# One PSUM bank in place of two for the phase sums, half a granule kept in the other, and a reordered first step and tail

## The chip, the core and the metric

The kernel runs on one core of a Trainium2 chip. The metric is the time of one execution in microseconds, as the device measures it. The engines are named as in the profile: PE (TensorE matmuls, PEld its weight loads), DVE (VectorE), ACT (ScalarE), POOL (GpSimd) and SP (SyncE, which here only issues transfers). Each engine works through its own instructions in the order in which the program puts them, and waits on semaphores for the others.

## The reference

Two branches are added to the input. A is an attention layer with a recurrent memory: 64 segments of 32 rows go through it one after the other, each behind 8 memory rows, which are the first 8 output rows of the segment before. B sends the two rows with the largest router score through a gated MLP.

```python
def _A_ref(x, mem0, Wq, Wk, Wv, Wo, seg_len):
    ...
    for s in range(n_seg):
        xs = x[:, s * seg_len:(s + 1) * seg_len, :].copy()
        h = jnp.concatenate([mem, xs], axis=1)
        q = jnp.einsum('btd,dhe->bhte', h, Wq)
        k = jnp.einsum('btd,dhe->bhte', h, Wk)
        v = jnp.einsum('btd,dhe->bhte', h, Wv)
        scores = jnp.einsum('bhqe,bhke->bhqk', q, k) * scale
        scores = jnp.where(mask[None, None], scores, -1000000000.0)
        p = _softmax(scores, axis=-1)
        o = jnp.einsum('bhqk,bhke->bhqe', p, v)
        o = jnp.einsum('bhte,hed->btd', o, Wo)
        mem = o[:, :M, :].copy()
        outs.append(o[:, M:, :])
...
xn = _layernorm(x, axis=-1)
return x + _A_ref(xn, A_mem0, A_Wq, A_Wk, A_Wv, A_Wo, A_seg_len) + _B_ref(xn, B_w_r, B_w_gate, B_w_up, B_w_down)
```

x is 1 x 2048 x 1024 in bf16, with 32 heads of 128; the MLP has 3584 hidden columns. The last 8 rows of a segment (called left rows here) and the first 24 are handled apart, since the left rows' queries, keys and values don't depend on the memory and can be computed for all segments at once, in the first step.

## The kernel before

The weights Wq, Wk, Wv and Wo are cut into 64 granules of 128 partitions by 2048 columns (512 KB). 44 of them stay in SBUF (`wres`, `W8A`, `W8B`, `XLT`); two and a half lie in PSUM, in the four tiles KEPT (granules 0, 7 and part of 27), and are copied into SBUF buffers BK just before they are read (`bring_back`, L404). The other 17 (`streamed`) are fetched again in every segment through five slots: `fetch` (L375) issues the transfer of the granule five places ahead when a granule has been read.

A segment's step runs six phases (L742): Q, K of the first 16 heads, Q, K of the second 16, V of the first, V of the second. A phase sums eight granules into a PSUM tile PSm (L745), four matmuls at a time on four column groups of PE; a group of four is the unit of pace in what follows. ACT copies PSm into XB (L754) or VM (L770), and the pool psA has two banks, so that the next phase begins in the other one at once. Three groups into the next phase PE turns XB (L632) into the buffer BT, from where ACT and DVE copy it to QT or KT (L637, L642).

The scores of a half (L650, L652) go to the bank BS after group 6 of phases 2 and 4. DVE adds the mask and subtracts the maximum (L659 to L665), ACT takes the exponential (L669), DVE divides by the sum and transposes (L674 to L685): `exponent` and `soften`. `attend` (L703, L706) multiplies by V, twice for each half; its sums lie in BT and, for the first half, in the second half of the bank that will hold WO. ACT copies them to OT and OTL (L712, L714). Then L350 puts the residual into WO, and 16 pairs of heads are projected into it (L789), with the attends of the second half ahead of pairs 5 and 8. L819 copies WO to XN, PE turns it into the memory columns of the next segment's ST (L340, L364), and the next step begins.

The places where such pieces of work go are written by hand: `hook(p, kc, fn)` runs fn after group kc of phase p. Within an engine the program keeps that order.

In the first step PE also computes the left rows' Q, K and V (`left_qk` L495, `left_v` L522), from PSUM tiles of the same two banks; the router's scores are 16 tiles of work on DVE (`router_tile`, L263 and L265), started after phase 0; the two rows with the largest scores are then picked and loaded (`router_top`, `route`) after phase 2. In the tail the left rows' attention is projected in two blocks (`left_rows_out`, L865), and the MLP's weights come in 46 pieces: 32 of gate and up, read by `gate_up` (L894), and 14 of down (L921). Each piece read frees the room for another.

Of the kernel before, what the change touches and what calls it, by code (L numbers as in the profile page):

```python
# [22 lines left out]
KEPT_HERE = (FIRST_KEPT, NEXT_KEPT, HALF_KEPT)  # L23
NEG = -30000.0
# [5 lines left out]
def kernel(  # L30
# [68 lines left out]

    def granule_out(t, g):  # L100
        return t[:, :] if g < 48 else t.rearrange("p (hh d) -> p hh d", hh=2)
# [7 lines left out]
    psA = ctx.enter_context(tc.tile_pool(name="psA", bufs=2, space=PSUM))  # L109
# [10 lines left out]
    wsc = {g: dram.tile([P, 2048], BF16, name=f"wsc{g}") for g in streamed}  # L120
# [106 lines left out]
    def left_turns():  # L227
        for t in range(4):
            PX = psA.tile([P, 1024], BF16, tag="acc", name="PX").rearrange("p (k t) -> p k t", k=KC)
# [56 lines left out]
    def route():  # L286
        T = home(hx, [P, 2048], BF16, "RT2")
        xs, T = T[0:2, 0:1024], T[:, 1024:2048]
        for c in range(2):
            v = nc.gpsimd.value_load(I8[0:1, c:c + 1], min_val=0, max_val=S - 1)  # L290
            routed_rows.append(v)
            nc.gpsimd.dma_start(out=xs[c:c + 1, :], in_=x2[bass.ds(v, 1), :])
        mv = T[0:2, 24:26].rearrange("p (t c) -> p t c", t=1)
# [81 lines left out]
    def fetch():  # L375
# [6 lines left out]
        else:  # L382
            nc.sync.dma_start(out=t[:, :], in_=wsc[g][:, :])
# [6 lines left out]
    def keep(g, t):  # L390
        for c, K in KEPT_COLS[g].items():
# [3 lines left out]
            XK = one.tile([P, 512], BF16, tag="bx", name="XK")  # L395
# [17 lines left out]
    def copy_block(g):  # L413
        nc.gpsimd.dma_start(out=granule_out(wsc[g], g), in_=granule_dram(g))
# [73 lines left out]
    def left_qk(mat, half, Gs, between, h0=0, h1=16):  # L488
# [3 lines left out]
        for h in range(h0, h1):  # L492
            PSG = psA.tile([P, 512], F32, tag="acc", name="PSG")
# [22 lines left out]
    def left_v(half, Gs):  # L516
        VG = home(hm, [P, 2048], BF16, "VG")
        for b in range(4):
            for jq in range(4):
                PSV = psA.tile([P, 512], F32, tag="acc", name="PSV")  # L520
# [22 lines left out]
    def left_done(p):  # L543
# [3 lines left out]
        if p == 0:  # L547
            spread(1, NT)
            for t in range(NT):
                router_tile(t)  # L550
        elif p == 1:
            router_out()
# [3 lines left out]
        elif p == 2:  # L556
            router_top()
            routed.append(route())
# [62 lines left out]
    for s in range(NSEG):  # L621
# [115 lines left out]

        for p, (mat, half) in enumerate(PHASES):
            PSm = psA.tile([P, 512], F32, tag="acc", name="PSm")
# [12 lines left out]
            if mat < 2:  # L752
                XB = one.tile([P, 512], BF16, tag=("bE", "kt")[mat], name="XB")
                nc.scalar.copy(out=XB[:, :], in_=PSm[:, :])  # L754
                hooks.setdefault((p + 1, 3), []).insert(0, lambda m=mat, h=half, b=XB: transposes(m, h, b))

                if s == 0:
                    Gs = [Gv_ for _, Gv_ in behind]
                    kept = (x for g_, Gv_ in behind if g_ in KEPT_COLS for x in keep(g_, Gv_))
                    if p == 0:  # L760
                        left_qk(mat, half, Gs, kept, 8, 13)
                        sd_rows(MV[:, 1:NT, :], VE[:, 1:NT])
                    elif p == 1:
                        left_qk(mat, half, Gs, kept, 0, 1)
                        nc.gpsimd.tensor_copy(out=GATE, in_=gathered[0][:, 0, 128:132])
                        copy_blocks(6)
                    left_qk(mat, half, Gs, kept, (13, 1)[p] if p < 2 else 0)
            else:
                VM[half] = one.tile([P, 512], BF16, tag="bA", name="VM")
                nc.scalar.copy(out=VM[half][:, :], in_=PSm[:, :])  # L770
# [6 lines left out]
        if s == 0:  # L777
            nxt["wo"] = psA.tile([P, 512], F32, tag="acc", name="WO")

        WO = nxt["wo"]  # L780
# [104 lines left out]
    GU = psA.tile([P, 512], F32, tag="acc", name="GU")  # L885
# [16 lines left out]
    early = len(pieces) + FC // 2 - len(moe)  # L902
# [60 lines left out]
```

## Time and profile before

| | |
|---|---|
| median of 3 runs | 1857.16 us (1852.51 to 1863.57) |
| profiled execution | 1853.95 us |
| its span, first to last instruction | 1852.3 us |
| PE busy | 1554.8 us, 84% |
| DVE busy | 880.0 us, 48% |
| ACT busy | 772.9 us, 42% |
| POOL busy | 320.9 us, 17% |
| moved by DMA | 678.50 MB, mean 366 GB/s |
| mean granted TensorE clock | 0.98 |

Busy shares are means over a first step of some 245 us, 63 like steps, and a tail of some 90 us. Rows of a timeline give the start in us, the duration, the engine, the line of the kernel, the operation with its output and inputs, their shapes, and in brackets how long the engine stood idle before it and who released it. A matmul's row lasts longer than its place in the pipeline: the next one starts before it ends.

### The profile page before, as it was taken

The page shows a single profiled execution, that of the slowest core. Times are in us where ns is not written, and L with a number is a line of the kernel's source. Part 1 is how long each engine was busy: PE and PEld are TensorE (multiplying, and loading weights), DVE is VectorE, ACT ScalarE, POOL GpSimd, SP SyncE. Part 2 cuts the span into 40 slices and gives each one's busy share as a digit, 9 for nine tenths or more (in the row PEclk, how much of TensorE's full clock was granted, in tenths as well). Part 3 has the DMA queues.
Part 4 walks back from the last instruction along what each step waited for, and adds up shares of the span by engine and source line. Part 5 has one row for each costly group of instructions (what it writes and reads, how often), then busy time and mean ns, then how long its engine had stood idle before and what let it go on. Part 6 is the DMA issues. An engine that isn't in the chain of part 4 may idle for free. (4 is left out here: it accounts for less than half of the span.)

```text
span 1852.3 us, 70387 instructions
## 1 busy us (share of the span) xinstructions
PE 1554.8 (84%) x30370; PEld 828.2 (45%) x30370; DVE 880.0 (48%) x2711; ACT 772.9 (42%) x2017; POOL 320.9 (17%) x592
## 2 busy tenths in 40 slices
PE   6879978888888888888888888888888888888888
PEld 3334434444444444444444444444444444444465
DVE  6721135555554444555555555545555455555420
ACT  3232134444444444444444444444444444444400
POOL 1120211111111111111111111111111111111200
PEclk9989989999999999999999999999999999999988
DMA  9692899999999999999999999999999999999996
GB/s 357 236 332 81 263 334 393 397 392 393 380 395 382 382 365 393 390 386 381 388 397 394 380 392 394 393 361 394 395 396 396 391 394 394 398 395 392 390 365 224
DMA packets 223288, 678.50 MB, mean 366 GB/s; under 512 B 46848, under 2 KB 54320, under 8 KB 222976
## 3 DMA queue, kind: packets, MB, share of 16 engines
q1 hardware_dynamic: 196768, 623.79, 87.8%
q0 software_dynamic: 24192, 46.54, 7.5%
q8 instruction: 237, 3.88, 0.8%
q10 hardware_dynamic: 2016, 3.67, 0.6%
q14 instruction: 75, 0.61, 0.1%
HBM read 652.90 MB, written 29.89 MB: 369 GB/s over the span
## 5 line engine op out<-in xcount | busy, mean ns | idle before, releaser
L745 PE MATMUL PSm<-wres,ST 128*32 128x512 bf16 x6400 | 500.8, 383 | 0.0
L745 PEld LDWEIGHTS <-ST 128*32 128x32 bf16 x12288 | 313.6, 96 | 333.1 <-issue 90.8
L745 PE MATMUL PSm<-g,ST 128*32 128x512 bf16 x3084 | 307.2, 384 | 32.9 <-DMA g<-wsc 27.2
L406 ACT COPY BK<-KEPT 128x512 bf16<-128x512 bf16 x315 | 189.3, 601 | 180.4 <-PE WO L789 70.4
L789 PEld LDWEIGHTS <-OT 128*32 128x32 bf16 x8192 | 209.0, 97 | 93.1 <-issue 77.4
L754 ACT CAST XB<-PSm 128x512 bf16<-128x512 f32 x256 | 150.3, 587 | 119.9 <-PE PSm L745 118.2
L642 DVE COPY KT<-BT 128x512 bf16<-128x512 bf16 x128 | 51.8, 405 | 287.4 <-PE BT L632 287.4
L789 PE MATMUL WO<-W8B,OT 128*32 128x256 bf16 x4096 | 185.7, 276 | 0.0
L745 PE MATMUL PSm<-W8A,ST 128*32 128x512 bf16 x2048 | 182.9, 380 | 0.0
L789 PE MATMUL WO<-g,OT 128*32 128x256 bf16 x2560 | 131.0, 278 | 58.9 <-DMA g<-wsc 52.3
L587 POOL DMA_DIRECT2D QKL<-ql_d x63 | 46.5, 739 | 750.3 <-ACT OTL L714 735.7
L823 POOL DMA_DIRECT2D out_dram<-XN x256 | 130.4, 525 | 183.3 <-DVE XN L819 183.0
L770 ACT CAST VM<-PSm 128x512 bf16<-128x512 f32 x128 | 80.2, 626 | 113.2 <-PE PSm L745 113.1
L406 DVE COPY BK<-KEPT 128x512 bf16<-128x512 bf16 x189 | 80.2, 424 | 72.5 <-ACT BK L406 36.9
L495 PE MATMUL PSG<-XLT,wres 128*128 128x512 bf16 x352 | 99.6, 385 | 12.1 <-ACT XB L754 12.1
L632 PEld LDWEIGHTS <-XB 128*128 128x128 bf16 x1024 | 58.0, 98 | 108.5 <-ACT XB L754 101.4
L632 PE MATMUL BT<-IDENT,XB 128*128 128x128 bf16 x1024 | 101.9, 222 | 3.6
L674 DVE TENSOR_REDUCE DN<-BS 128x8 f32<-128x320 f32 x128 | 62.9, 492 | 84.1 <-ACT BS L669 84.1
L637 ACT COPY QT<-BT 128x512 bf16<-128x512 bf16 x128 | 75.0, 586 | 54.8 <-PE BT L632 52.6
L659 DVE TENSOR_TENSOR BS<-BS,CT 128x96 f32<-128x96 f32 (+1 forms) x256 | 59.6, 233 | 76.5 <-PE BS L652 72.0
L745 PE MATMUL PSm<-BK,ST 128*32 128x512 bf16 x567 | 76.5, 389 | 22.2 <-DVE ST L364 22.2
L819 DVE CAST XN<-WO 128x256 bf16<-128x256 f32 x64 | 27.2, 425 | 137.3 <-PE WO L789 137.3
(171 smaller groups left out, 2278.2 us busy)
## 6 DMA issues: line engine op xcount, KB each, us to landing
g<-wsc SPq DMA_DIRECT2D x1071, 512.0 KB, 6.3
ql_d<-GA POOLq DMA_DIRECT2D x16, 512.0 KB, 5.7
QKL<-ql_d POOLq DMA_DIRECT2D x63, 128.0 KB, 6.3
MW<-in_B_w_gate_dram SPq DMA_DIRECT2D x16, 448.0 KB, 7.9
MW<-in_B_w_down_dram SPq DMA_DIRECT2D x14, 512.0 KB, 9.8
wres<-in_A_Wk_dram SPq DMA_DIRECT2D x12, 512.0 KB, 10.3
MW<-in_B_w_up_dram SPq DMA_DIRECT2D x12, 448.0 KB, 8.5
XP<-in_A_x_dram SPq DMA_DIRECT2D x8, 512.0 KB, 10.2
```

The costliest lines, as they stand in the source:

```text
L406: copy(out=back[g][c], in_=KEPT_COLS[g][c])
L495: nc.tensor.matmul(PSG[:, :], lhsT=part(Gs[kc], h // 4)[:, P * (h % 4):P * (h % 4 + 1)], rhs=XLT[:, :, kc, :], start=(kc == 0), stop=(kc = ...
L632: nc.tensor.transpose(out=PTq[:, il, :, :].rearrange("p j r -> p (j r)"), in_=XB[:, il * P:(il + 1) * P], identity=IDENT[:, :])
L637: nc.scalar.copy(out=QT[half][:, :, :], in_=pv)
L642: nc.vector.tensor_copy(out=KT[half][:, :, 0:32], in_=pv)
L659: nc.vector.tensor_tensor(out=S4, in0=S4, in1=m, op=ALU.add)
L674: nc.vector.tensor_reduce(out=DN[:, :], in_=S8, axis=AX.X, op=ALU.add)
L745: nc.tensor.matmul(PSm[32 * jq:32 * jq + 32, :], lhsT=ST[:, kc, :], rhs=part(Gv, jq), start=(kc == 0), stop=(kc == KC - 1), tile_position= ...
L754: nc.scalar.copy(out=XB[:, :], in_=PSm[:, :])
L770: nc.scalar.copy(out=VM[half][:, :], in_=PSm[:, :])
L789: nc.tensor.matmul(PS[32 * g:32 * g + 32, 0:256], lhsT=lhs(h), rhs=Gv[:, D * hs + 256 * g:D * hs + 256 * (g + 1)], start=False, stop=(last ...
L823: nc.gpsimd.dma_start(out=out2[s * SEG:s * SEG + XM, 256 * g:256 * (g + 1)], in_=OB[32 * g:32 * g + XM, :])
```

## The change

Five things change.

1. The banks of psA become two named tiles, a0 and a1. In the first step the sums alternate between them as before; from the second step on, all six phases and WO use a0 (`accumulator`).
2. PSm is copied out in two halves of 256 columns, the first by ACT, the second by DVE, for XB as for VM. Some work for PE moves between the phases (`between`): Q's transposes go from the middle of K's phase to its end, the scores of the first half behind phase 2. The attends of the first half move from groups 3 and 6 of phase 5 to groups 5 and 7, and their sums use BS in every step.
3. From the second step on, a1 holds half of granule 45 (KEPT4). Only the other half, 128 x 1024, is copied to scratch and streamed; in each step DVE and ACT copy the kept columns into the same slot (`kept_piece`, in phase 4). In the first step the two kept blocks are turned twice by PE, with ACT between, to get into PSUM (`keep`).
4. In the first step the router's 16 tiles move from behind phase 0 to behind the third head of phase 1; the router's output row, the loading of the two rows and their normalisation move one place later as well, `route` to behind the eighth head of phase 3.
5. In the tail, 20 instead of 26 of the 32 gate and up pieces are read ahead of the second block of left rows.

```diff
+HALF_STREAMED = 45
+    def accumulator(shape, dtype, name, both):
+        sums_of[0] = (sums_of[0] + 1) % 2 if both else 0
+        return psA.tile(shape, dtype, tag=f"a{sums_of[0]}", name=name)
...
-    psA = ctx.enter_context(tc.tile_pool(name="psA", bufs=2, space=PSUM))
+    psA = ctx.enter_context(tc.tile_pool(name="psA", bufs=1, space=PSUM))
...
-            nc.sync.dma_start(out=t[:, :], in_=wsc[g][:, :])
+            nc.sync.dma_start(out=t[:, 0:columns(g)], in_=wsc[g][:, :])
...
+    def kept_piece(c, copy):
+        t = [t for q, t in queued if q == HALF_STREAMED][0]
+        copy(out=t[:, 512 * c:512 * (c + 1)], in_=KEPT_COLS[HALF_STREAMED][c])
...
-                    if s > 0:
-                        nxt["wo"] = psA.tile([P, 512], F32, tag="acc", name="WO")
...
-                sums[half] = [BS[:, 0:4 * NK] if half or s == 0 else nxt["wo"][:, 256:256 + 4 * NK], OPB]
+                sums[half] = [BS[:, 0:4 * NK], OPB]
...
-        hook(2, 6, lambda: scores(0))
         if s > 0:
-            hook(2, 7, lambda: bring_back(HALF_KEPT, 3, "kt", nc.scalar.copy))
+            hook(3, 0, lambda: bring_back(HALF_KEPT, 3, "kt", nc.scalar.copy))
+            hook(4, 1, lambda: kept_piece(2, nc.vector.tensor_copy))
+            hook(4, 2, lambda: kept_piece(3, nc.scalar.copy))
         hook(3, 4, exponent)
         hook(3, 4, lambda: soften(0))
...
-        hook(*((5, 0) if s else (4, 7)), exponent)
-        hook(*((5, 0) if s else (4, 7)), lambda: soften(1))
-        hook(5, 3, lambda: attend(0, 0))
-        hook(5, 6, lambda: attend(0, 1))
+        if s > 0:
+            hook(5, 0, exponent)
+            hook(5, 0, lambda: soften(1))
+        hook(5, 5, lambda: attend(0, 0))
+        hook(5, 7, lambda: attend(0, 1))
+        hook(4, 6, lambda: scores(1))
+
+        def between(p):
+            if p == 2:
+                scores(0)
+            elif p == 4 and s == 0:
+                exponent()
+                soften(1)
+            elif p % 2 == 1:
+                turned_q.pop()()
...
-            PSm = psA.tile([P, 512], F32, tag="acc", name="PSm")
+            PSm = accumulator([P, 512], F32, "PSm", s == 0)
...
-                nc.scalar.copy(out=XB[:, :], in_=PSm[:, :])
-                hooks.setdefault((p + 1, 3), []).insert(0, lambda m=mat, h=half, b=XB: transposes(m, h, b))
+                nc.scalar.copy(out=XB[:, 0:256], in_=PSm[:, 0:256])
+                nc.vector.tensor_copy(out=XB[:, 256:512], in_=PSm[:, 256:512])
+                turn_it = lambda m=mat, h=half, b=XB: transposes(m, h, b)
+                if mat == 0:
+                    turned_q.append(turn_it)
+                else:
+                    hooks.setdefault((p + 1, 3), []).insert(0, turn_it)
+                if p > 0:
+                    between(p)
...
-                nc.scalar.copy(out=VM[half][:, :], in_=PSm[:, :])
+                nc.scalar.copy(out=VM[half][:, 0:256], in_=PSm[:, 0:256])
+                nc.vector.tensor_copy(out=VM[half][:, 256:512], in_=PSm[:, 256:512])
...
+            KEPT.append(psA.tile([P, 1024], BF16, tag="a1", name="KEPT4"))
...
-    early = len(pieces) + FC // 2 - len(moe)
+    early = len(moe)
```

How the instructions stand on the engines is shown at three places; the words in brackets are the semaphores of the engines (or DMA queues) that an instruction waits for, without the value. Line numbers of the changed kernel lie some 15 to 40 above those of before.

PE, from phase 0 to phase 1 of a later step: the last rows of phase 0, which read a granule kept in PSUM (BK), and the first of phase 1 (a resident granule). Before:

```order
L745 MATMUL PSm<-BK,ST 32x512 [waits DVE_49]
L745 LDWEIGHTS ST
L745 MATMUL PSm<-BK,ST 32x512 [waits Activation_49]
L745 LDWEIGHTS ST
L745 MATMUL PSm<-wres_217,ST 32x512 [waits PE_49]
```

and in the change:

```order
L771 MATMUL PSm<-BK,ST 32x512 [waits DVE_49]
L771 LDWEIGHTS ST
L771 MATMUL PSm<-BK,ST 32x512 [waits Activation_49]
L771 LDWEIGHTS ST
L771 MATMUL PSm<-wres_217,ST 32x512 [waits DVE_49]
```

The first matmul of phase 1 waited for PE itself and now waits for DVE; the first matmuls of phases 2 to 5 and of WO do the same.

DVE, from the maximum of the first half's scores (NM, BS) through the softmax (DN, PT, PL) to the K copy of the second half (KT). Before:

```order
L665 TENSOR_TENSOR BS<-BS,NM 128x320 [waits DVE_49]
L674 TENSOR_REDUCE DN<-BS 128x8 [waits Activation_49]
L675 RECIPROCAL DN<-DN 128x8 [waits DVE_49]
L680 TENSOR_TENSOR PT_2469<-BS,DN 128x256 [waits DVE_49,PE_49]
L681 TENSOR_TENSOR PL<-BS,DN 128x4x2x8
L684 STREAM_TRANSPOSE PT_2469<-PT_2469 128x256 [waits DVE_49]
L685 STREAM_TRANSPOSE PT_2469<-PL 128x256 [waits DVE_49]
L642 COPY KT<-BT 128x16x32 [waits PE_49,Activation_49]
```

and in the change:

```order
L680 TENSOR_TENSOR BS<-BS,NM 128x320 [waits DVE_49]
L689 TENSOR_REDUCE DN<-BS 128x8 [waits Activation_49]
L690 RECIPROCAL DN<-DN 128x8 [waits DVE_49]
L695 TENSOR_TENSOR PT_2493<-BS,DN 128x256 [waits DVE_49,PE_49]
L696 TENSOR_TENSOR PL<-BS,DN 128x4x2x8
L699 STREAM_TRANSPOSE PT_2493<-PT_2493 128x256 [waits DVE_49]
L700 STREAM_TRANSPOSE PT_2493<-PL 128x256 [waits DVE_49]
L781 CAST XB<-PSm 128x256 [waits Activation_49]
L434 COPY g<-KEPT_2063 128x512 [waits DMAHW7_49,DMAHW2_49,DMAHW1_49]
L657 COPY KT<-BT 128x16x32 [waits DVE_49,PE_49,Activation_49]
```

Two instructions have come between the softmax and the K copy: DVE's half of phase 3's sums, which waits for ACT, and the copy of a kept piece of granule 45.

DVE, the same place for the second half. Before:

```order
L664 TENSOR_REDUCE NM<-BS 128x8 [waits DVE_49]
L665 TENSOR_TENSOR BS<-BS,NM 128x320 [waits DVE_49]
L674 TENSOR_REDUCE DN<-BS 128x8 [waits Activation_49]
L675 RECIPROCAL DN<-DN 128x8 [waits DVE_49]
L680 TENSOR_TENSOR PT_2583<-BS,DN 128x256 [waits DVE_49]
```

and in the change:

```order
L679 TENSOR_REDUCE NM<-BS 128x8 [waits DVE_49]
L680 TENSOR_TENSOR BS<-BS,NM 128x320 [waits DVE_49]
L813 CAST VM<-PSm 128x256 [waits DMASW3_49,Activation_49]
L689 TENSOR_REDUCE DN<-BS 128x8 [waits Activation_49]
L690 RECIPROCAL DN<-DN 128x8 [waits DVE_49]
L695 TENSOR_TENSOR PT_2617<-BS,DN 128x256 [waits DVE_49]
```

DVE's half of VM[0], the sums of phase 4, now stands between the maximum and the softmax; the other half of VM, of phase 5, stands behind the softmax.

More of the change, by code (lines that the diff above doesn't have):

```diff
@@ L118, with columns @@
     ol_d = [dram.tile([16, P, XL * H], BF16, name=f"ol_d{t}") for t in range(4)]
-    wsc = {g: dram.tile([P, 2048], BF16, name=f"wsc{g}") for g in streamed}
+    def columns(g):
+        return 1024 if g == HALF_STREAMED else 2048
+    wsc = {g: dram.tile([P, columns(g)], BF16, name=f"wsc{g}") for g in streamed}
     r_d = dram.tile([1, S], BF16, name="r_d")
@@ L292, in route @@
             nc.gpsimd.dma_start(out=xs[c:c + 1, :], in_=x2[bass.ds(v, 1), :])
+        routed.append(T)
+    def route():
+        T = routed.pop()
+        xs, T = T[0:2, 0:1024], T[:, 1024:2048]
         mv = T[0:2, 24:26].rearrange("p (t c) -> p t c", t=1)
@@ L413, in copy_block @@
     def copy_block(g):
-        nc.gpsimd.dma_start(out=granule_out(wsc[g], g), in_=granule_dram(g))
+        src = granule_dram(g)
+        nc.gpsimd.dma_start(out=granule_out(wsc[g], g), in_=src if g >= 48 else src[:, 0:columns(g)])
+    def kept_piece(c, copy):
+        t = [t for q, t in queued if q == HALF_STREAMED][0]
+        copy(out=t[:, 512 * c:512 * (c + 1)], in_=KEPT_COLS[HALF_STREAMED][c])
     to_copy = list(streamed)
@@ L492, in left_qk @@
         for h in range(h0, h1):
[L493 removed]
+            PSG = accumulator([P, 512], F32, "PSG", True)
             for kc in range(KC):
@@ L546, in left_done @@
                 fetch()
[L547 to L552, printed above, removed]
+        if p == 1:
             area("big0", [P, 8, 2048], "W8A")
@@ L557, in left_done @@
             router_top()
-            routed.append(route())
+            route_rows()
         elif p == 3:
```

47 lines of the change are left out of this document (31 added, 16 removed).

## The prediction

> **What bounds the kernel now.** I read the page first, then the line L819, which runs once a segment, the waits, and the timelines of PE, ACT and DVE over whole steps.
>
> ```profile
> span 1852.3 us, 70387 instructions
> g<-wsc SPq DMA_DIRECT2D x1071, 512.0 KB, 6.3
> ...
> L819 DVE CAST XN<-WO x64: 423/425/426, 245.1 to 1762.1; 128x256 bf16<-128x256 f32 x64
> ...
> 300.00:1700.00 1400.00, 1182.01 (x26140) 630.09 (x26136) 710.99 (x2274) 652.77 (x1750) 258.45 (x467) 1.00 1.01 389
> ...
> PE WO L789 <- DMA g<-wsc: 52.3, 100, 2.2
> PE PSm L745 <- DMA g<-wsc: 27.2, 69, 1.2
> ```
>
> L819 ends each segment's step, so a step is (1762.1 - 245.1) / 63 = 24.08 us; the first step and its set-up take 245 us, the tail 90. In the third row (busy times of PE, PE loads, DVE, ACT, POOL, then clock, DMA share, GB/s) the DMA engines are never idle and move 389 GB/s, 9.37 MB a step, of which the 17 granules are 8.9. The transfers set the pace, but by little, as one step on PE shows:
>
> ```profile
> 1019.05 0.40 PE L745 MATMUL PSm<-BK,ST 128*32 128x512 bf16 x4 [0.35 <-DVE ST L364]
> 1021.58 0.39 PE L745 MATMUL PSm<-BK,ST 128*32 128x512 bf16 x3
> 1025.33 0.40 PE L632 MATMUL BT<-IDENT,XB 128*128 128x128 bf16 x4
> 1025.66 0.40 PE L745 MATMUL PSm<-wres,ST 128*32 128x512 bf16 x4
> 1026.10 0.39 PE L745 MATMUL PSm<-wres,ST 128*32 128x512 bf16 x4
> 1026.32 0.21 PE L650 MATMUL BS<-KT,QT 128*32 128x40 bf16 x4
> 1032.01 0.21 PE L650 MATMUL BS<-KT,QT 128*32 128x40 bf16 x4 [0.45 <-DVE KT L642]
> 1036.41 0.31 PE L350 MATMUL WO<-XS,IDENT 128*32 128x256 bf16 x4 [0.21 <-ACT OTL L714]
> 1044.20 0.40 PE L745 MATMUL PSm<-BK,ST 128*32 128x512 bf16 x4 [0.35 <-DVE ST L364]
> 1050.68 0.21 PE L650 MATMUL BS<-KT,QT 128*32 128x40 bf16 x4
> 1056.37 0.21 PE L650 MATMUL BS<-KT,QT 128*32 128x40 bf16 x4 [0.69 <-DVE KT L642]
> ```
>
> I cut the step into four: A from phase 0 to the first scores (L650), B to the second scores, C to the residual matmul (L350), D to the next phase 0. B is 5.69 us in both steps here (1026.32 to 1032.01, 1050.68 to 1056.37), and a wait for DVE ends it, not one for a DMA: a chain through ACT and DVE, from the scores over the softmax to the next scores, that no transfer shortens. The two waits for g add up to 79.5 us, 1.3 us a step. So there is at most a few us a step between the transfers' pace and that of the chain PE-ACT-DVE, and what lengthens the chain by more comes out in full.
>
> **The change, part by part.** *The handoff.* From step 1 on all phases and WO share the bank a0. The first matmul of each phase waits for DVE, whose half of the copy waits for ACT alone; since nothing else tells DVE that the matmuls are done, ACT's half is what it waits for. The two halves run one behind the other.
>
> ```profile
> 1022.08 0.59 ACT L754 CAST XB<-PSm 128x512 bf16<-128x512 f32 x1 [1.94 <-PE PSm L745]
> 1038.11 0.27 ACT L712 CAST OT<-BS 128x128 bf16<-128x128 f32 x1 [1.02 <-PE BT L706]
> ```
>
> ACT takes 0.59 us for 512 columns and 0.27 for 128; on the line between them, 0.38 for 256. DVE's 256 columns are L819's 0.425. Gaps: matmul end to ACT 0.11 (1021.58 + 0.39 to 1022.08); ACT to DVE 0.04 and DVE to PE 0.06 (rows below: 1028.96 + 0.43 to 1029.43; 1031.57 + 0.38 to 1032.01). From the last group of four matmuls to the next phase: 0.39 + 0.11 + 0.38 + 0.04 + 0.43 + 0.06 = 1.41 us, where the pace was 0.22 (1026.10 to 1026.32). Each free handoff costs PE 1.19 us. Not shown is a bank read by both engines; were the halves side by side, a handoff would take 0.42 less (0.38 + 0.04), and that end is kept as a rival.
>
> [...]
>
> *DVE's queue.* DVE works in order, and its half of phase 3's copy stands behind the whole softmax of the first half, its half of VM[0] behind the mask and maximum of the second. These are the prices:
>
> ```profile
> 1026.82 0.27 DVE L659 TENSOR_TENSOR BS<-BS,CT 128x96 f32<-128x96 f32 x1 [0.56 <-PE BS L652]
> 1028.17 0.50 DVE L665 TENSOR_TENSOR BS<-BS,NM 128x320 f32<-128x320 f32 x1
> 1028.96 0.43 ACT L669 ACTIVATE BS<-BS 128x320 f32<-128x320 f32 x1
> 1029.43 0.49 DVE L674 TENSOR_REDUCE DN<-BS 128x8 f32<-128x320 f32 x1 [0.76 <-ACT BS L669]
> 1031.20 0.45 DVE L685 STREAM_TRANSPOSE PT<-PL 128x256 bf16<-128x256 bf16 x1
> 1031.57 0.38 DVE L642 COPY KT<-BT 128x512 bf16<-128x512 bf16 x1
> 1034.86 0.49 DVE L674 TENSOR_REDUCE DN<-BS 128x8 f32<-128x320 f32 x1 [0.49 <-ACT BS L669]
> 1035.96 0.21 DVE L681 TENSOR_TENSOR PL<-BS,DN 128x64 bf16<-128x64 f32 x1
> ```
>
> Masks begin 0.50 us after the scores and take 1.85 (1026.82 to 1028.67); exponential 0.43 with 0.04 on either side; softmax 2.22 (1029.43 to 1031.65), of which BS is free after 1.31 (1034.86 to 1036.17).
>
> A, new: 24 groups x 0.22 = 5.28, one set of K transposes 0.33 (1025.33 to 1025.66; Q's now lie in the handoff of phase 1), two handoffs 2.38. **A = 8.0** (7.27 here, 6.48 in the next step).
>
> B, new: phase 2's copy into XB takes the buffer that the scores still read as QT, so ACT starts at 0.50 and DVE ends at 1.35; phase 3 starts at 1.41 and would be over near 3.4. Masks 1.35 to 3.20, exponential to 3.67, softmax 3.71 to 5.93, DVE's half of phase 3 to about 6.28 (DVE starts the next independent instruction 0.08 early, 1031.57 against 1031.65), phase 4 at 6.34. PE stands still for almost 3 us. Then seven groups 1.54, transposes 0.33, K copied meanwhile: **B = 8.25**, 2.56 more. The copy of granule 45's kept piece (DVE, a copy of 512 columns, 0.38 by the KT row; ACT 0.6) lies in the first groups of phase 4 where DVE and ACT are free: nothing, or 0.4 a step without that cover.
>
> C, new: masks end at 2.35, DVE's half of VM[0] at 2.78, phase 5 at 2.84 (it followed at once before). Six groups to 4.16; BS, which now takes the first sums in place of WO's second half, is free at 2.35 + 0.04 + 0.43 + 0.04 + 1.31 = 4.17; attend(0,0) at 4.23. The rest from these rows:
>
> ```profile
> 1037.74 0.24 PE L703 MATMUL BS<-PT,VL 32*128 32x160 bf16 x1
> 1034.74 0.27 ACT L712 CAST OT<-WO 128x128 bf16<-128x128 f32 x1
> 1035.26 0.22 PE L703 MATMUL WO<-PT,VL 32*128 32x160 bf16 x1 [0.71 <-ACT OTL L714]
> 1036.42 0.67 ACT L770 CAST VM<-PSm 128x512 bf16<-128x512 f32 x1
> ```
>
> An attend's first copy starts 0.37 later (1037.74 to 1038.11), the next attend 0.52 after that (1034.74 to 1035.26), ACT's VM copy 1.16 after that (1035.26 to 1036.42). WO must now wait for this copy: 4.23 + 0.89 + 1.16 + 0.46 (ACT's half, 0.08 of it in the copy before) + 0.04 + 0.43 + 0.06 = 7.27. **C = 7.27** against 4.40, 2.87 more.
>
> D keeps its work. A step with little waiting:
>
> ```profile
> 480.16 0.31 PE L350 MATMUL WO<-XS,IDENT 128*32 128x256 bf16 x4 [0.21 <-ACT OTL L714]
> 484.44 0.39 PE L789 MATMUL WO<-wres,OT 128*32 128x256 bf16 x8
> 485.08 0.40 PE L789 MATMUL WO<-g,OT 128*32 128x256 bf16 x8 [0.25 <-DMA g<-wsc]
> 486.65 0.40 PE L745 MATMUL PSm<-BK,ST 128*32 128x512 bf16 x4 [0.35 <-DVE ST L364]
> ```
>
> 6.49 us, less 0.42 for the late g (0.64 in place of 0.22): **D = 6.07**.
>
> The step: 8.0 + 8.25 + 7.27 + 6.07 = **29.6 us**, 5.5 more than 24.08; over 63 steps +348 us.
>
> *The stream* loses 0.262 MB: 9.37 - 0.26 = 9.11 MB, 23.4 us at 389 GB/s. Behind a step of 29.6 us the transfers idle a fifth of the time, and a fetch is issued five granules ahead; in the densest stretch, D, granule 58, fetched when 41 is read early in phase 5 (3.1 us into C), is used 3.1 us into D, 7.3 us later, against a median of 6.3 us to landing under full load. I put 0 for late granules, with 1 us a step as the upper end.
>
> *First step and tail.*
>
> ```profile
> 136.78 1.44 PE L495 MATMUL PSG<-XLT,wres 128*128 128x512 bf16 x3 [12.14 <-ACT XB L754]
> L265 DVE CUSTOM_DVE_ANT_0 XR<-XR,MISC 128x1024 bf16<-128x1024 bf16 x16 | 19.6, 1225 | 0.5
> 1790.71 6.08 PE L894 MATMUL GU<-RXT,MW 128*128 128x2 bf16 x233
> 1799.44 2.14 PE L894 MATMUL GU<-RXT,MW 128*128 128x2 bf16 x75 [2.66 <-issue]
> 1807.40 9.33 PE L865 MATMUL WD<-W8B,OTA 128*128 128x512 bf16 x32
> ```
>
> The 12.1 us in which PE waited for ACT, itself held by the routing, should go, since route() now follows eight heads of phase 3. Against it: the 16 router tiles start three heads (24 matmuls, 5.2 us) later on DVE and hold up phase 2's K copy by about as much; two pieces of granule 45 are turned twice, some 1.5 us each by the rows of copy and transposes. Net -3, between -12 and +10. In the tail 20 pieces instead of 26 go ahead of the second block of rows: of their 280 matmuls 233 are done before 1799.44, and 47 more at 28.5 ns (2.14 us / 75) take 1.3 us, so the block starts at 1800.8 and not at 1807.4; 84 matmuls come behind instead, 84 x 28.5 ns = +2.4. Net -4, between -7 and +2.
>
> **Sum.** 1852.3 + 348 - 3 - 4 = 2193 us of span; the profiled execution took 1853.95 in all and the median of the runs, 1857.16, is 4.9 above that span: **2198 us**.
>
> **The rivals.**
>
> *The stream sets the pace after all, faster.* If the handoffs fitted into the time PE now waits, a step would be 23.4 us, 63 x 0.68 = 43 us less, and with first step and tail about 1807 us. For it speaks the DMA share of 1.01. It decides as long as the chain stays under 23.4 us; against it B alone, 5.69 us and no DMA in it, gets a DVE copy and a phase start behind the softmax. Chance 0.03.
>
> *The halves overlap.* If what DVE waits for is older work of ACT, the handoffs after phases 0, 1, 2 and 5 are 0.42 shorter each, 1.7 us: a step of 27.9, some 107 us less, 2091. DVE's queue stalls phases 4 and 5 all the same. The first matmul's wait for DVE alone speaks against it. Chance 0.06.
>
> *Late granules on top.* Where PE's stalls bunch the demand in D, the full 1 us or more is added, with the copy into granule 45's slot waiting for a landing: 31 us or above, 2285. The lead of 7.3 us speaks against it. Chance 0.08.
>
> *No change*, by errors that cancel: 0.01.
>
> **How the numbers follow.** The forecast has 0.82. Its own range is 29.0 to 30.3 us a step, 2160 to 2245. For eight in ten I reach down to the overlapping halves and up to half of the late granules: 2090 to 2265. Runs of this kernel tell about 0.5% from no change, so faster by more than that 0.03, within 0.01, slower 0.96.
>
> **What would show it.** In the new timeline: DVE's copy of PSm starting some 0.04 us after ACT's; PE idle for about 3 us ahead of phase 4 with DVE as releaser, 2 us ahead of phase 5, B near 8.2 and C near 7.3; waits for g almost gone, the DMA share near 0.8 at 305 GB/s; no 12 us gap near 125 us. The prediction is wrong if DMA share stays at 1.0, if the halves start together, or if phase 4 starts before the softmax is over.

## The result, and the profile after

The changed kernel takes 2394.82 us (median of 4 runs, 2388.92 to 2406.59) against 1859.51 us for the kernel before, measured beside it: ratio 1.288, 95% interval 1.284 to 1.293. The forecast was 2198 us, 2090 to 2265. The direction was right; the time is 197 us above the forecast and outside the range. The profiled execution took 2390.68 us.

The page of the changed kernel gives its span:

```profile
span 2389.0 us, 71366 instructions
```

The line that ends each step (L819 before, L866 now):

```profile
L866 DVE CAST XN<-WO x64: 424/425/426, 253.9 to 2303.1; 128x256 bf16<-128x256 f32 x64
```

A step is (2303.1 - 253.9) / 63 = 32.53 us, where 24.08 was measured before and 29.59 forecast. The first step ends 8.8 us later than before (253.9 against 245.1), the tail is 2389.0 - 2303.1 = 85.9 us, 4.3 less. So of the 197 us the steps hold 63 x 2.94 = 185, and the first step 12.

The waits of PE in the changed kernel (sum in us, times, longest):

```profile
PE PSm L771 <- DVE XB L781: 322.6, 252, 2.9
PE PSm L771 <- DVE VM L813: 127.8, 63, 2.1
PE WO L365 <- DVE VM L813: 95.4, 63, 1.5
PE PSm L771 <- DMA g<-wsc: 17.6, 31, 1.7
```

The wait for granules fell from 79.5 to 17.6 us; in its place PE waits 545.8 us for DVE's halves. One step on the timeline, first the copies of ACT and DVE, then PE (phase 0 ends with the group at 1199.88, phase 3 at 1209.7; the first scores stand at 1206.31, the second at 1216.03):

```profile
1206.88 0.37 ACT L780 CAST XB<-PSm 128x256 bf16<-128x256 f32 x1 [1.03 <-PE BS L667]
1207.28 0.42 DVE L781 CAST XB<-PSm 128x256 bf16<-128x256 f32 x1 [1.26 <-ACT XB L780]
...
1211.72 0.45 DVE L700 STREAM_TRANSPOSE PT<-PL 128x256 bf16<-128x256 bf16 x1
1212.09 0.39 DVE L781 CAST XB<-PSm 128x256 bf16<-128x256 f32 x1
...
1199.88 0.38 PE L771 MATMUL PSm<-HP,ST 128*32 128x512 bf16 x1
1201.29 0.83 PE L771 MATMUL PSm<-wres,ST 128*32 128x512 bf16 x12 [0.94 <-DVE XB L781]
1206.31 0.19 PE L665 MATMUL BS<-KT,QT 128*32 128x40 bf16 x4
1209.05 0.62 PE L771 MATMUL PSm<-wres,ST 128*32 128x512 bf16 x8
1212.53 1.04 PE L771 MATMUL PSm<-W8A,ST 128*32 128x512 bf16 x8 [2.54 <-DVE XB L781]
1213.34 0.66 PE L771 MATMUL PSm<-g,ST 128*32 128x512 bf16 x4
1213.77 0.66 PE L771 MATMUL PSm<-W8A,ST 128*32 128x512 bf16 x4
1215.73 0.47 PE L771 MATMUL PSm<-W8A,ST 128*32 128x512 bf16 x4
1216.03 0.19 PE L665 MATMUL BS<-KT,QT 128*32 128x40 bf16 x4
1218.75 0.40 PE L771 MATMUL PSm<-W8A,ST 128*32 128x512 bf16 x4 [2.08 <-DVE VM L813]
1219.48 1.10 PE L771 MATMUL PSm<-wres,ST 128*32 128x512 bf16 x8
1220.33 0.68 PE L771 MATMUL PSm<-g,ST 128*32 128x512 bf16 x4
1224.26 0.31 PE L365 MATMUL WO<-XS,IDENT 128*32 128x256 bf16 x4 [1.52 <-DVE VM L813]
```

The chain is the one that was forecast: phase 1 starts 1.41 us after phase 0's last group, DVE's half starts 0.03 us after ACT's (1207.28 against 1206.88 + 0.37), phase 4 starts 6.22 us after the first scores (forecast 6.34) because DVE's half stands behind the softmax, phase 5 2.72 after the second (2.84). What was not forecast stands behind the 2.54 us wait: four matmuls take 0.43 us (1213.34 to 1213.77) in place of 0.22. After some 3.2 us, near 1215.7, the pace is back, and behind the next wait, from 1219.2 on, it is halved again. Such a stretch at half pace is called a dip below.

The windows view over many steps, and about over the segments B, C and D of this step and A of the next (busy us of PE, PE loads, DVE, ACT, POOL; granted clock, DMA share, GB/s):

```profile
300.00:1700.00 1400.00, 976.34 (x19300) 522.02 (x19300) 644.33 (x1985) 449.30 (x1338) 190.79 (x344) 0.88 0.82 280
...
1206.50:1215.00 8.50, 4.94 (x90) 2.24 (x76) 4.73 (x14) 2.64 (x6) 0.18 (x1) 0.85 0.65 224
1215.00:1224.00 9.00, 5.66 (x100) 2.33 (x99) 4.73 (x14) 2.84 (x12) 0.00 (x0) 0.76 0.72 207
1224.00:1230.30 6.30, 5.18 (x156) 3.89 (x155) 3.35 (x14) 2.28 (x7) 1.12 (x2) 1.00 0.90 304
1230.30:1238.30 8.00, 6.44 (x108) 3.07 (x112) 2.13 (x5) 2.65 (x6) 2.21 (x6) 1.00 1.02 387
```

The granted clock fell from 1.00 to 0.88, and it falls in B and C (0.85 and 0.76 in this step), where PE waits. And the DMA share of 0.82 is a mean over unlike stretches: in the step shown 0.65 in B, 1.02 at 387 GB/s in A, where the transfers have no reserve.

Cut into the prediction's segments (PE's timeline, 61 steps; least, mean in us):

| kernel | A | B | C | D |
|---|---|---|---|---|
| before | 5.94, 6.54 | 5.69, 5.75 | 4.39, 4.47 | 6.49, 7.23 |
| forecast | 8.0 | 8.25 | 7.27 | 6.07 |
| after | 7.94, 8.55 | 8.18, 8.71 | 7.21, 8.13 | 6.06, 7.08 |

The least values are the forecast's to 0.07 us; the means are 2.9 us a step above it. So the question for the runs was not where PE waits, but what makes the rest longer than its best case.

### The profile page after: what moved, and what is told of

The parts are those of the page before. It is cut to its first block, busy times and chain, and to the rows that moved or that the text cites. A ratio compares the mean times of both kernels' runs of the same rounds, so it can differ in the third digit from the quotient of the medians.

```text
span 2389.0 us, 71366 instructions
## 1 busy us (share of the span) xinstructions
PE 1706.9 (71%) x30374; PEld 909.7 (38%) x30386; DVE 1054.3 (44%) x3158; ACT 727.2 (30%) x2084; POOL 321.7 (13%) x592
## 4 chain that ended last, share of the span: by engine, by line
PE 54%; DVE 19%; DMA 15%; ACT 7%; issue 4%; SPq 0%; DVEq 0%; POOL 0%; ACTq 0%
PE PSm L771 27%; DMA g<-wsc 11%; PE WO L836 10%; DVE XB L781 4%; PE PSG L515 4%; ACT XB L780 3%; DVE NM L679 3%; DVE VM L813 2%; DVE BS L674 2%; PE BS L716 2%; PE BT L647 2%; PE PSV L542 2%; DVE BS L676 1%; ACT OTL L727 1%; DVE BS L680 1%
## 5 line engine op out<-in xcount | busy, mean ns | idle before, releaser
L771 PE MATMUL PSm<-W8A,ST 128*32 128x512 bf16 x2048 | 229.7, 453 | 288.2 <-DVE XB L781 160.4
L771 PE MATMUL PSm<-g,ST 128*32 128x512 bf16 x3084 | 350.7, 437 | 19.7 <-DMA g<-wsc 17.6
L781 DVE CAST XB<-PSm 128x256 bf16<-128x256 f32 x256 | 106.2, 415 | 349.6 <-ACT XB L780 349.6
L836 PEld LDWEIGHTS <-OT 128*32 128x32 bf16 x8192 | 236.1, 109 | 34.9 <-issue 6.8
L836 PE MATMUL WO<-W8B,OT 128*32 128x256 bf16 x4096 | 228.0, 327 | 0.0
L725 ACT CAST OT<-BS 128x128 bf16<-128x128 f32 x256 | 68.1, 266 | 429.3 <-PE BT L719 366.7
L780 ACT CAST XB<-PSm 128x256 bf16<-128x256 f32 x256 | 95.7, 374 | 294.3 <-PE PSm L771 225.0
L813 DVE CAST VM<-PSm 128x256 bf16<-128x256 f32 x128 | 53.7, 420 | 168.2 <-ACT VM L812 168.2
L684 ACT ACTIVATE BS<-BS 128x320 f32<-128x320 f32 x128 | 54.0, 422 | 187.9 <-DVE BS L680 187.9
L725 DVE CAST OT<-BT 128x128 bf16<-128x128 f32 x128 | 37.3, 292 | 127.3 <-PE BT L719 111.8
```

The lines of the kernel that those rows point to most:

```text
L725: copy(out=OT[half][:, 2 * ph + jl, :, :], in_=ov[:, :, 0:SEG])
L771: nc.tensor.matmul(PSm[32 * jq:32 * jq + 32, :], lhsT=ST[:, kc, :], rhs=part(Gv, jq), start=(kc == 0), stop=(kc == KC - 1), tile_position= ...
L780: nc.scalar.copy(out=XB[:, 0:256], in_=PSm[:, 0:256])
L781: nc.vector.tensor_copy(out=XB[:, 256:512], in_=PSm[:, 256:512])
L813: nc.vector.tensor_copy(out=VM[half][:, 256:512], in_=PSm[:, 256:512])
L836: nc.tensor.matmul(PS[32 * g:32 * g + 32, 0:256], lhsT=lhs(h), rhs=Gv[:, D * hs + 256 * g:D * hs + 256 * (g + 1)], start=False, stop=(last ...
```

## The experiments

Theory 1: the waits lower PE's clock, and the matmuls behind them run at half pace. Rivals: granules that are late in A; a further wait in the order of the hooks. The ratio of each run is to the kernel before, measured beside it; that kernel took 1858.55 to 1865.03 us there, so differences in us to the change, which was measured apart from the runs, are good to some 6 us.

**PE kept busy.** Ahead of phases 4 and 5, where PE stands still, it multiplies an identity into a part of BT that nobody reads.

```diff
+        def fill(n):
+            for _ in range(n):
+                nc.tensor.matmul(BT[:, 416:512], lhsT=IDENT[:, :], rhs=IDENT[:, 0:96], start=True, stop=True, ...)
...
+                if s > 0 and p == 3:
+                    fill(24)
...
+                    if s > 0:
+                        fill(24)
```

> The changed kernel with 24 matmuls of 128 x 96 columns that nobody reads put on PE ahead of phase 4 and again ahead of phase 5, into unused columns of the bank BT, from the second step on. They should fit into the two long stalls (2.54 and 2.08 us in the changed kernel's timeline). Theory 1, the stalls drop PE's clock and the groups behind them run at 0.43 us in place of 0.22: granted clock from 0.88 to 0.95 or more, a step from 32.5 to 29.5-30.3 us, 2195 to 2250 us in all, although PE does more work. Theory 2, the 2.9 us a step beyond the forecast are late granules or slow transfers: no gain, 2395 us or more. Theory 3, PE's own instruction stream limits the groups: slower by the 48 extra matmuls, some 2 us a step, 2500 us.

2297.73 us, 97 less than the change; clock 0.967. B 8.20 and C 7.21 on average, equal to their least values in the changed kernel: work added to PE made it faster, so the half pace in B and C came from the waits. The step is 30.99 us, above the 29.5 to 30.3 expected, and the time above 2195 to 2250, since A rose to 8.90 and D stayed at 6.65. PE's timeline in this run, ahead of phase 4 and in an A:

```profile
1200.20 1.18 PE L764 MATMUL BT<-IDENT 128*128 128x96 bf16 x24 [0.75 <-ACT QT L652]
1201.99 0.61 PE L776 MATMUL PSm<-W8A,ST 128*32 128x512 bf16 x8 [0.61 <-DVE XB L786]
1202.42 0.40 PE L776 MATMUL PSm<-g,ST 128*32 128x512 bf16 x4
1202.63 0.40 PE L776 MATMUL PSm<-W8A,ST 128*32 128x512 bf16 x4
...
1217.46 0.39 PE L776 MATMUL PSm<-g,ST 128*32 128x512 bf16 x4
1219.34 0.62 PE L776 MATMUL PSm<-g,ST 128*32 128x512 bf16 x4 [1.07 <-DMA g<-wsc]
1219.72 1.09 PE L776 MATMUL PSm<-wres,ST 128*32 128x512 bf16 x8
```

Behind the fill the pace is 0.21 us. In A a granule comes 1.07 us late, and the pace behind it is halved again (eight matmuls in 1.09 us, where they took 0.61).

**The shorter waits filled too.** The same, with more of it ahead of phases 1, 2 and 3 and of WO.

```diff
+                if s > 0 and p < 3:
+                    fill(12)
...
+        if s > 0:
+            fill(12)
         WO = accumulator([P, 512], F32, "WO", False)
```

> The run with unread matmuls ahead of phases 4 and 5, with 12 more of them in each of the waits ahead of phases 1, 2 and 3 and ahead of WO (0.6 us at full clock, inside waits of 1.0 to 1.5 us). It had A at 8.9 us on average against 7.94 at least, D 6.65 against 6.06. Theory 1, what is left there is the clock again, that falls after the shorter waits: A 8.0 to 8.4, D 6.1 to 6.3, a step of 29.7 to 30.3 us in place of 31.0, 2215 to 2255 us, clock 0.98 or above. Theory 2, it is late granules (37.8 us of waits in all): A stays at 8.7 or above, a step of 30.8 to 31.2, 2285 to 2310 us. Theory 3, the fill delays the copies' release: 31.5 us or more.

2333.01 us, clock 0.978, a step of 31.6 us. D fell from 6.65 to 6.29, as theory 1 had it. A rose to 9.85, its least value to 8.67: the fill ahead of phase 3 is in front of the first scores and costs its 0.7 us there (theory 3). A's excess over its least value stayed near 1 us (1.18), although the clock was at half for only 44 us of all its steps (491 us in the changed kernel), so it isn't the clock behind the handoffs.

**Granules made smaller.** In the run of the first fill, and in the changed kernel, the six streamed granules of phases 0 to 2 are fetched as halves, and the first half is multiplied in place of the second.

```diff
-        return 1024 if g == HALF_STREAMED else 2048
+        return 1024 if g == HALF_STREAMED or g < 24 else 2048
...
+                half_read = s > 0 and g < 24 and g in streamed
...
- rhs=part(Gv, jq),
+ rhs=part(Gv, jq % 2 if half_read else jq),
```

> The run with unread matmuls ahead of phases 4 and 5, in which the six streamed granules of phases 0 to 2 are fetched from the second step on as their first half, which is multiplied twice in place of both halves: the same matmuls, 1.57 MB a step less. It had a step of 31.0 us (A 8.9 on average). Theory 1, what is left above 29.5 us comes from granules that are late in A, where the DMA engines are at full share (387 GB/s), and from the half clock that follows such a wait: A 8.0 to 8.2 us, D 6.1 to 6.4, a step of 29.5 to 29.9 us, 2200 to 2230 us. Theory 2, it is the handoffs' own waits: A 8.7 or above, a step of 30.7 to 31.1, 2280 to 2310 us.

> The changed kernel with the same six granules halved and no fill. Theory 1, the clock falls after the waits ahead of phases 4 and 5 whatever the transfers do: B and C stay at 8.5 to 8.8 and 8.0 to 8.3 us, A falls to 8.0 to 8.3, a step of 31.6 to 32.3 us, 2335 to 2385 us. Theory 2, the late granules start it: with none, B is 8.2 and C 7.2 in most steps, a step of 29.5 to 30.5 us, 2200 to 2270 us.

With the fill: 2278.67 us. Theory 1 was right for A, 7.95 on average and 8.01 at most, with no wait for a granule left. But D is 7.36 in place of 6.1 to 6.4, and the step 30.8. PE's timeline there shows why; the wait ahead of WO now starts a dip in most steps:

```profile
1170.38 0.41 PE L365 MATMUL WO<-XS,IDENT 128*32 128x256 bf16 x4 [1.51 <-DVE VM L821]
1170.55 1.10 PE L846 MATMUL WO<-W8B,OT 128*32 128x256 bf16 x16
1171.40 0.67 PE L846 MATMUL WO<-g,OT 128*32 128x256 bf16 x8
```

Without the fill: 2389.71 us, 5 less than the change, which the spread of the runs does not tell from nothing. A falls to 7.97, B rises to 9.03 and D to 7.49: the granules' lateness is worth nothing by itself here, because the clock takes it back elsewhere (at half for 577 us of the steps, for 491 in the changed kernel). Expected were 2335 to 2385.

**All three together.** The filled run with small granules, and unread matmuls ahead of WO.

```diff
+        if s > 0:
+            fill(12)
         WO = accumulator([P, 512], F32, "WO", False)
```

> The run with halved granules and unread matmuls ahead of phases 4 and 5, with 12 more unread matmuls ahead of WO. Without these it had A 7.95, B 8.20 and C 7.21 us in every step and D at 7.36 on average, 6.06 at least. Theory 1, D's excess is the half clock that follows the wait of 1.5 us ahead of WO: D 6.1 to 6.3 in nearly every step, a step of 29.4 to 29.7 us, span 2190 to 2210 us, clock above 0.97; then the sum of the prediction holds for a chain at full clock with no late granule, and all that the changed kernel takes above it is these two. Theory 2, D's excess is something else: D stays above 7 us, 2270 us or more.

2219.12 us, clock 0.986; A 7.96, B 8.20, C 7.21, D 6.33 on average, D 6.07 in the median step. The span, 2217.1 us, is 7 above the range expected. Line ends and window of this run:

```profile
L878 DVE CAST XN<-WO x64: 423/425/425, 254.2 to 2131.4; 128x256 bf16<-128x256 f32 x64
```

```profile
300.00:1700.00 1400.00, 1076.16 (x23978) 655.32 (x23976) 704.85 (x2173) 490.96 (x1463) 208.03 (x376) 1.00 0.78 253
```

At clock 1.00 a step takes (2131.4 - 254.2) / 63 = 29.80 us, the forecast's 29.59 and 0.2. So the waits and their lengths were right. Of the 185 us that the steps take above them, this run removes 63 x (32.53 - 29.80) = 172: it takes away the half clock and the waits for granules together. Those waits came to 17.6 us in the changed kernel, so most of the 172 is half clock, with late granules as one of its triggers; the other 13 us are the 0.2 a step that the forecast was short at full clock.

**Which part of the change makes the waits.** Four runs undo parts: ACT alone empties the bank; two banks alternate in every step, with granule 45 streamed whole; both; and the softmax of the first half is put behind DVE's half.

```diff
-                nc.scalar.copy(out=XB[:, 0:256], in_=PSm[:, 0:256])
-                nc.vector.tensor_copy(out=XB[:, 256:512], in_=PSm[:, 256:512])
+                nc.scalar.copy(out=XB[:, :], in_=PSm[:, :])
```

```diff
-            PSm = accumulator([P, 512], F32, "PSm", s == 0)
+            PSm = accumulator([P, 512], F32, "PSm", True)
...
-        WO = accumulator([P, 512], F32, "WO", False)
+        WO = accumulator([P, 512], F32, "WO", True)
```

```diff
-        hook(3, 4, lambda: soften(0))
+        hook(4, 0, lambda: soften(0))
```

> The changed kernel, but ACT alone empties PSm, 512 columns at once; one bank as in the change. If the long stalls come from DVE's place in the chain (its halves queued behind the softmax and behind the maximum), the waits of 2.54 us ahead of phase 4 and 2.08 ahead of phase 5 go, B falls from 8.2 (9.7 at the low clock) to about 5.75, C to about 7.0, each free handoff takes 1.15 us instead of 1.41, a step 26.3 to 27.5 us: 1990 to 2070 us, with the clock at 0.94 or more. If instead the single bank is what costs, and not the second engine, hardly anything changes: 2300 us or more.

> The changed kernel with two banks for the sums in every step, so without the kept half: granule 45 is streamed whole again. Two engines still empty each bank, and the reordered first step, attends and tail stay. If waiting for the one bank is the main cost: phases follow one another without a handoff, a step is 24.3 to 25.5 us, the DMA share goes back to about 1, 1880 to 1960 us. If the order of DVE's queue costs as much by itself, through the scores of the second half: B about 6.7 instead of 5.69 stays, but hidden in part. If the rest of the reordering is the cost: 2200 us or more.

> The changed kernel with both the shared bank and the second engine undone (two banks alternate in every step, all of granule 45 is streamed, ACT alone copies 512 columns): of the segments' work only the moved hooks are left, that is the second softmax and the attends, the first attention sums in BS in place of WO's bank, and the transposes between the phases. Theory 1, the moved hooks have a price of their own, which the wait of the attends for BS (2.3 us before each first attend of C with two banks) shows: a step of 25.5 to 27 us, 1950 to 2040 us, with C still 5.5 us or above where the kernel before had 4.4. Theory 2, only bank and engines cost: the gains of 3.75 us (ACT alone) and 4.3 us (two banks) a step add up, 32.5 - 8.0 = 24.5 us a step, 1870 to 1900 us.

> The changed kernel with one line moved: DVE's softmax of the first half is put behind phase 3's copies instead of ahead of them, so that DVE's half of phase 3 runs as soon as the masks are done. If DVE's queue holds phase 4 back, phase 4 starts some 2 us earlier, its stall of 2.54 us shrinks to about 0.8, B goes from 8.2 (at full clock) to about 6.9, and with a better clock a step is 29 to 31 us: 2170 to 2300 us. If what holds phase 4 back is ACT or the bank itself, B stays at 8.2 or above: 2390 us.

| kernel | us | ratio, 95% | clock | A | B | C | D |
|---|---|---|---|---|---|---|---|
| ACT alone | 2138.86 | 1.136 to 1.152 | 0.933 | 7.99 | 6.29 | 6.97 | 7.48 |
| two banks | 2123.24 | 1.133 to 1.148 | 0.927 | 8.08 | 7.25 | 5.72 | 7.15 |
| both | 1997.62 | 1.068 to 1.078 | 0.943 | 8.13 | 5.51 | 5.70 | 7.16 |
| softmax behind | 2308.35 | 1.228 to 1.245 | 0.896 | 8.25 | 7.61 | 7.98 | 7.42 |

The first two were expected faster than they came (1990 to 2070, 1880 to 1960), priced at full clock again. Of ACT alone the fastest step, 26.8 us, lies in the 26.3 to 27.5 expected, the mean at 28.8, though B is 6.28 at least where 5.75 was expected; of two banks even the fastest, 26.9, lies above the 24.3 to 25.5, so something besides the clock was left out there: in that run PE waits 96.2 us for DVE's half of XB ahead of the transposes and 97.2 us for BS ahead of the first attends, 1.5 us a step each. The single bank and the second engine each cost some 4 us a step beside the other (step 32.5 to 28.2 and to 28.8), and 2.3 and 1.7 us with the other gone (to 26.5), half clock included. With both undone it is still 26.5 us and 7% slower than before, as its theory 1 had it: the moved hooks have a price of their own. In that run's timeline the first attend of C waits for BS, which the change lets it use in place of WO's bank, and its waits name the granules:

```profile
1156.25 0.22 PE L716 MATMUL BS<-PT,VL 32*128 32x160 bf16 x1 [2.28 <-DVE PL L696]
```

```profile
PE BS L716 <- DVE PL L696: 128.2, 63, 2.3
PE PSm L769 <- DMA g<-wsc: 97.2, 159, 2.4
```

C is 5.70 there against 4.47 before, and A 8.13 against 6.54, with most of the waits for granules; that the transfers which PE leaves unused in C are what it lacks in A is argued, not shown. With the softmax behind DVE's half, one B in the timelines of PE and DVE:

```profile
1150.74 0.61 PE L771 MATMUL PSm<-W8A,ST 128*32 128x512 bf16 x8 [0.72 <-DVE XB L781]
1153.92 0.21 PE L665 MATMUL BS<-KT,QT 128*32 128x40 bf16 x4 [1.04 <-ACT KT L655]
...
1152.30 0.45 DVE L700 STREAM_TRANSPOSE PT<-PL 128x256 bf16<-128x256 bf16 x1
1152.98 0.41 DVE L657 COPY KT<-BT 128x512 bf16<-128x512 bf16 x1
```

The wait ahead of phase 4 falls by 1.8 us, from 2.54 to 0.72, so that wait was DVE's order; but B at its least falls by only 0.6 (8.18 to 7.59), where 1.3 was expected (8.2 to 6.9), since the copy of K now stands behind the softmax and the scores wait. The whole was expected at 2170 to 2300 us and came just above.

**The first step.** It ends 8.8 us later than before, where 3 us less were forecast. PE's timeline of the changed kernel there:

```profile
53.96 1.01 PE L515 MATMUL PSG<-XLT,g 128*128 128x512 bf16 x2 [15.17 <-DVE XB L781]
...
111.06 0.24 PE L665 MATMUL BS<-KT,QT 128*32 128x40 bf16 x4 [6.52 <-ACT KT L655]
```

The second row is the forecast's delay of the K copy, 6.5 us for 5.2. The first was not seen: DVE's half of phase 0's sums stands behind older work of DVE, the row statistics of the other tiles, with which DVE is busy from 29.9 us until that copy starts at 53.5. One run lets ACT copy that one bank alone.

```diff
+                if s == 0 and p == 0:
+                    nc.scalar.copy(out=XB[:, :], in_=PSm[:, :])
+                else:
```

> The changed kernel, but ACT alone copies the sums of phase 0 in the first step; all else as in the change. The changed kernel had a first step that ended at 253.9 us with a wait of 15.2 us for DVE's half of that copy. Theory 1, DVE's half stands behind the row statistics of the other tiles, and that wait is new time: the end of the first step falls by 12 to 16 us, to 238 to 242 us, the whole to 2378 to 2384 us. Theory 2, the row statistics are needed soon after and the wait moves to another place: 250 us or more, the whole within 4 us of 2394.8.

2381.91 us, 13 less than the change; the first step ends at 242.2, 11.7 earlier, against the 12 to 16 expected. Without that wait it is 2.9 us shorter than the kernel before's: the forecast's -3.

**The parts that help, alone.** The kernel before with the change's tail order; and with that and the routing split as in the change (its rows asked for where the routing stood, as they also are in the change; only its arithmetic moves, behind eight heads of phase 3).

```diff
-    early = len(pieces) + FC // 2 - len(moe)
+    early = len(moe)
...
-            routed.append(route())
+            route_rows()
...
+                    elif p == 3:
+                        left_qk(mat, half, Gs, kept, 0, 8)
+                        routed.append(route())
```

> The kernel before with the tail's order alone (as many pieces ahead of the second block of rows as the change puts there). The changed kernel's tail is 4.3 us shorter than that of the kernel before. Theory 1, that is the reordering: -3 to -5 us, ratio 0.997 to 0.9985. Theory 2, it comes from an earlier end of transfers behind longer steps: 0 to -1 us.

> The kernel before with the tail's order and with the routing's arithmetic put behind eight heads of phase 3, as in the change, but the router's tiles left where they were, one bank pair and ACT alone in all steps. Theory 1, the wait of 12.1 us in the first step goes and nothing takes its place: first step 8 to 12 us shorter, tail 4, ratio 0.991 to 0.994, the version that beats both. Theory 2, the routing is late for the rows that it gathers or DVE holds up phase 3's heads: the first step gains 0 to 4 us, ratio 0.996 to 0.998.

The tail alone: 1855.81 us, ratio 0.998, interval 0.996 to 1.001, which leaves the two theories open; in its profile the tail is 84.7 us against 90.2. With the routing: 1849.45 us, ratio 0.993, interval 0.989 to 0.996, within the 0.991 to 0.994 expected: a small gain of 0.7%, but faster than both kernels. Its first step, which ends 13.0 us earlier than before where 8 to 12 were expected, and its PE at the place where 12.14 us were waited before:

```profile
L827 DVE CAST XN<-WO x64: 424/425/426, 232.1 to 1758.2; 128x256 bf16<-128x256 f32 x64
```

```profile
142.32 0.81 PE L500 MATMUL PSG<-XLT,wres 128*128 128x512 bf16 x3 [0.72 <-ACT GA L502]
```

## Why the prediction was right and wrong

- *The bound and the direction.* Right: the transfers had little reserve over the chain PE-ACT-DVE, and the lengthened chain sets the pace; DMA share 0.82 for the 0.8 forecast, 280 GB/s for 305, waits for granules 17.6 us.
- *The handoff, 1.41 us; the halves in series.* Right: 1.41 us from the last group of phase 0 to phase 1, and DVE 0.03 us behind ACT. The rival of overlapping halves is out.
- *DVE's queue.* Right: waits of 2.54 and 2.08 us for "almost 3" and 2.
- *The step that failed* is the pace: "24 groups x 0.22 = 5.28" and "seven groups 1.54", and WO's matmuls, took every group at full clock behind waits that the same text put at 2 to 3 us. The sum of 29.6 us holds at full clock (29.80 with the waits filled and the granules small); the kernel takes 32.53. The half clock comes in stretches of 3.41 us, 144 of them in the 63 steps, some 2.3 a step; one costs 1.0 to 1.5 us (in the step shown B is 9.72 for 8.18, C 8.23 for 7.21).
- *The trace of before had the row.* There the clock was 0.99 over the steps (245 to 1762 us), but the two longest waits for a granule, 1.9 and 2.2 us, were followed by half pace. One of them on PE's timeline of the kernel before:

```profile
1232.89 0.40 PE L789 MATMUL WO<-W8B,OT 128*32 128x256 bf16 x8
1235.17 0.62 PE L789 MATMUL WO<-g,OT 128*32 128x256 bf16 x8 [1.88 <-DMA g<-wsc]
1237.30 0.64 PE L789 MATMUL WO<-wres,OT 128*32 128x256 bf16 x8
1237.73 0.64 PE L789 MATMUL WO<-g,OT 128*32 128x256 bf16 x8
```

  0.43 us a group (1237.30 to 1237.73) after a wait of 1.88, where 0.22 is usual. So the price of half pace could be read before the result. How often it would come could not: with two stretches a step, a number known from the trace of after alone, 2.0 to 3.0 us, the sum would have been 2324 to 2387 us.
- *Late granules, put at 0.* Right for the kernel as it is (small granules alone gain 5 us, which the spread does not tell from nothing), though not for the reason given: A runs at DMA share 1.02, and once the clock is held the late granule costs 0.95 us a step there (A 8.90 to 7.95).
- *Kept pieces, 0.* The copies stand in free stretches of both engines in the timeline; no run had them alone.
- *First step, -3.* The 12 us gap went and the K copy's delay came as forecast; the wait of 15.2 us for DVE's half was missed, by asking what DVE's queue holds at phases 3 and 4 and not at phase 0 of the first step.
- *Tail, -4.* Right: -4.3 in the profile.
- *The adding up.* B's terms, 6.34 + 1.54 + 0.33, give 8.21 and not 8.25, and the first step's, -12.1 + 5.2 + 3, give some -4 and not -3; both are small beside the 185 us.

## What to carry to other kernels

Here a stall cost more than its length where matmuls followed it, 0.43 us a group for 0.22 behind the waits of 2.54 and 2.08 us and 1.0 to 1.5 us a dip: look in the trace for the pace behind the longest waits before pricing them at full clock. Splitting a copy over two engines gained nothing, since the halves ran in series (0.37 and 0.42 us with 0.03 between, where ACT took 0.59 for the whole), and each half then waits in its engine's queue (in the first step PE stood still for 15.2 us behind DVE's); ask for every place, the first step's too, what stands ahead of it there. A mean DMA share, 0.82 here, hides the stretch in which the transfers are full, 1.02 in A, so read it by stage.

## What the runs showed of the hardware

A matmul group ran at 0.22 or 0.43 us: of 2365 spacings of neighbouring groups in the phases of the changed kernel's steps 1980 are 0.20 to 0.24 us, 286 are 0.40 to 0.45, and 89 lie between. The granted clock in the traces of the two kernels has only the values 1.00 and 0.50, and in each of the two all its changes lie on one grid of 3.41 us, to 0.002 us. In the steps of the changed kernel there are 95 spells of half clock, 62 of them 3.41 us long and the others two to four times that, 491 us in all. Four neighbouring cells of the grid in the step shown (windows view as above):

```profile
1209.05:1212.47 3.42, 0.95 (x16) 0.44 (x9) 2.76 (x9) 1.20 (x3) 0.00 (x0) 1.00 0.85 301
1212.47:1215.88 3.41, 3.35 (x32) 1.28 (x35) 0.76 (x3) 0.88 (x2) 0.00 (x0) 0.50 0.26 48
1215.88:1219.30 3.42, 1.34 (x56) 0.70 (x50) 2.48 (x7) 0.79 (x2) 0.00 (x0) 1.00 0.81 253
1219.30:1222.71 3.41, 3.41 (x48) 1.23 (x38) 1.61 (x6) 0.77 (x4) 0.00 (x0) 0.50 0.65 186
```

A cell in which PE is busy for 0.95 us is followed by half clock, one with 3.35 by full clock, one with 1.34 by half clock again. So it goes through the changed kernel's steps (262 to 2300 us): of the cells at full clock, half clock followed 71 of the 72 in which PE was busy for less than 40%, 24 of the 52 between 40 and 55%, and none of the 329 above. What counted in this trace is how little PE does within one cell, and so how a wait lies on the grid. The 63 waits ahead of phase 4, of 2.53 to 2.89 us, show it: the 30 of which 1.88 us or more fell into one cell were followed by half clock in the next cell, the 33 with 1.85 or less were not. The share itself is no sharp rule, since between 40 and 55% it went both ways, 24 to 28; and no run moved the grid against the steps.

Counted by waits of the changed kernel, 55 of the 63 ahead of phase 5 (2.1 us) had half pace within the next six rows of the timeline, 36 of 63 ahead of WO (1.5 us), 30 of the 64 for XB of 2.3 us and more, nearly all ahead of phase 4, and 5 of the 127 for XB of about 1 us. So length alone does not decide: a step is no whole number of cells, so the same wait lies differently from step to step. And taking one trigger away let another fire (D rose from 6.65 to 7.36 when A's late granules were gone).

From the second step on the longest wait of PE in the changed kernel was 2.89 us, less than a cell of 3.41 us, and the clock was 0.88.
